# Another hand-ordered task list for sparse attention followed by a squared-ReLU MLP

## Chip, core and metric

The kernel runs on one core of one Trainium2 chip. The metric is the device time of one execution in microseconds (us), lower is better. The core's engines each work through their own instruction queue in order: TensorE (PE in the profile, its weight loads PEld), VectorE (DVE), ScalarE (ACT), GpSimd (POOL) and SyncE (SP, which here only issues DMAs). Engines wait for each other by semaphores.

## What is computed

```python
scores = scale * np.matmul(q, k.transpose(0, 1, 3, 2))      # q, k, v: 4 x 8 x 768 x 64, f32
mask = np.abs(blk_i - blk_j) <= window                      # blocks of 32 tokens, window 1
mask = mask | (blk_i == 0) | (blk_j == 0) | (blk_i == n_blocks - 1) | (blk_j == n_blocks - 1)
for qb in range(n_blocks):
    for kb in sampled_blocks[qb]:                           # 3 drawn blocks for each block of queries
        mask[qb * block:(qb + 1) * block, kb * block:(kb + 1) * block] = True
scores = np.where(mask, scores, -1000000000.0)
attn = np.exp(scores - np.max(scores, axis=-1, keepdims=True))
attn = attn / (np.sum(attn, axis=-1, keepdims=True) + 1e-09)
x = np.matmul(attn, v).transpose(0, 2, 1, 3).reshape(3072, 512)
h = x @ w_in                                                # 512 x 2048
r = np.maximum(h, 0.0)
out = (r * r) @ w_out                                       # 2048 x 512
```

## The kernel before

**Units and batches.** Two heads of one batch entry make a unit, so there are 16 units (0 to 15), four to a batch entry. Batches 0 and 1 (units 0 to 7) compute all scores and apply the mask; batches 2 and 3 (units 8 to 15) compute only the blocks that the mask keeps, for which drawn blocks of keys are copied together (`k_gather`) and drawn blocks of values are fetched from a copy in HBM (`v_store`, `v_gather`, `v_window`).

**Attention.** For a unit, q and k are loaded in f32 (`load`, line 145), cast to bf16 (`cast_qk`), and transposed: in batch 0 on PE (`transp`, then `evac` out of PSUM), from batch 1 on by a transposing DMA (`transp_dma`, line 311). `scores` makes the products of keys and queries in PSUM, `exps` the exponentials on ACT (line 360), `masks` multiplies by the mask on DVE (line 367), `values` multiplies by v on PE. `normalize` divides by the sum, and `x_transp` with `x_evac`, or a DMA, turns the result into columns. In batch 0 the first 256 queries of each unit have the mask added in PSUM instead, as a product of `oh` and `R2`; `R2` is made by `mask_rows` on PE (line 258) and copied by `mask_rows_evac`, and it needs the table `bm` (line 249).

**MLP.** The tokens go in 12 tiles of 256. For each, `hidden` makes 512 hidden columns at a time (f = 0, 4, 8, 12) in four parts, `relu` (line 727 on ACT, 729 on DVE) and `square` (738 on ACT, 740 elsewhere) follow, `output` sums over all hidden columns in eight parts, `out_copy` copies to SBUF and `store` writes to HBM. The last tile's rows are stored in four pieces.

**Weights.** `w_load` fetches w_in and w_out in four parts each with cast to bf16, by DMAs that GpSimd issues (lines 328 and 331). Hidden columns f need part f / 4 of w_in; output parts need w_out parts in turn. `loads_gate` (line 338) makes the sync queue wait for w_out parts 2 and 3 before it starts the loads of batch 1.

**Order.** All of this is a list of 1224 tasks, made in the program's order and numbered from 0. A string, `PROGRAM`, says in which order they are issued and on which engine: `P`, `V`, `A`, `G`, `S` for PE, DVE, ACT, GpSimd and the sync queue, then the task's number, and for a task that takes a cell of PSUM the cell (0 to 3). Semaphores follow from the data. So each engine's queue is the subsequence of its letter, and the place of a word among words of other letters says nothing. Buffers are handed out in rotation in the order of the words (8 for exponentials, 3 for relus, 12 for squares).

Numbers that matter here: 0, 2 `mask_rows`; 1, 3 `mask_rows_evac`; 4 to 17 `keep_warm` (products of ones, as filler); 21 `table_load`; 22 `table_places`; 73 and 52 `cast_v` of units 3 and 1; 74 to 77 `w_load` of w_in parts 0 to 3; 78 to 81 `w_load` of w_out parts 0 to 3; 82, 83 `loads_gate`; 102 the first `scores`; 253 to 283 loads, casts and transposes of batch 1; 285 to 291 the first `scores` of batch 1; 774 to 777 `hidden` f = 0 of the first tile and 778 its `relu`; 781 to 784 `hidden` f = 4 and 785 its `relu`; 802 to 809 the first tile's `output`; 1184 to 1223 the last tile's `output`, `out_copy` and `store`.

Of the kernel before, what the change touches and what calls it, by code (L numbers as in the profile page):

```python
# [25 lines left out]
def kernel(  # L26
# [65 lines left out]
    def run_program(bufs):  # L92
        names = {"P": "PE", "V": "DVE", "A": "ACT", "G": "POOL", "S": "SP"}
        taken = {name: [] for name in bufs}
        cells = [None] * NX
        for word in PROGRAM.split():
            t = tasks[int(word[1:].partition("/")[0])]
            if t.blocks and names[word[0]] in t.blocks[1]:
                wanted[names[word[0]]].append(t.blocks[0])
        for word in PROGRAM.split():  # L100
            i, _, spot = word[1:].partition("/")
# [951 lines left out]
```

## Time and profile before

| | |
|---|---|
| time, median of 3 runs (lowest, highest) | 258.85 us (258.25, 259.73) |
| the profiled execution | 258.04 us, span 256.3 us |
| granted clock of TensorE over the span | 1.0 |
| HBM read, written | 35.51 MB, 7.91 MB |

The page gives busy time by engine first. A window's row shows each engine's busy time in that stretch with the number of its instructions, then the clock, the mean share of the 16 DMA engines, and GB/s. In a timeline, a row is a start, a length and an instruction; the bracket holds the idle time of its engine before it and what ended it. Line 203 is a helper that issues most matmuls, and lines 121 and 123 are one that issues copies, so those rows are told apart by their tiles. Matmuls overlap: their mean length is a latency, not a pitch.

### The profile page before, as it was taken

Reading aid. Unit: us, or ns where it says so; the run is one execution under the profiler, and the core shown is the slowest. Engines: PE = TensorE matmul, PEld = TensorE weight load, DVE = VectorE, ACT = ScalarE, POOL = GpSimd, SP = SyncE. Lnnn points to the kernel's source line nnn. Section 1 sums busy time; section 2 is a strip of 40 time slices with the busy share of each in tenths; the row PEclk is TensorE's granted clock in tenths of the full one; section 3 lists DMA queues with packets and bytes.
Section 4 is the critical chain, followed back from the end, with each engine's and each line's share of the span. In section 5 each row is a group of like instructions: output and inputs, shape, how many; then the busy total and the mean of one; then the engine's idle time right before and its main releaser. Section 6 shows DMA issues by size and latency. Waiting matters only on the chain.

```text
span 256.3 us, 12057 instructions
## 1 busy us (share of the span) xinstructions
PE 244.4 (95%) x5265; PEld 183.4 (72%) x5265; DVE 173.0 (67%) x411; ACT 183.4 (72%) x217; POOL 100.3 (39%) x178
## 2 busy tenths in 40 slices
PE   7988999989999999998999999999999999999994
PEld 5667779759975579975866766857774677666674
DVE  7678997789998999869939647656636725730301
ACT  3799999978999799946695975585965186623640
POOL 3264228002407006198558424174448620413100
PEclk9999999999999999999999999999999999999999
DMA  6999998999799997999589899996484922034122
GB/s 191 364 246 205 206 208 128 252 255 241 190 262 232 207 239 141 313 217 201 191 232 207 226 170 212 251 190 186 115 203 98 195 47 50 16 102 145 46 84 84
DMA packets 64692, 47.08 MB, mean 184 GB/s; under 512 B 31567, under 2 KB 60624, under 8 KB 64640
## 3 DMA queue, kind: packets, MB, share of 16 engines
q1 hardware_dynamic: 58512, 37.82, 63.0%
q0 software_dynamic: 5440, 8.05, 16.9%
q8 instruction: 41, 0.67, 1.2%
q10 hardware_dynamic: 688, 0.46, 0.6%
q14 instruction: 11, 0.09, 0.2%
HBM read 35.51 MB, written 7.91 MB: 169 GB/s over the span
## 4 chain that ended last, share of the span: by engine, by line
PE 68%; DMA 16%; DVE 4%; POOL 4%; SPq 3%; issue 2%; ACT 1%; DVEq 0%; POOLq 0%
PE X L203 63%; DMA w_out_sb<-in_moe_w_out_dram 5%; PE X L673 5%; DMA ys<-in_v_dram 3%; DMA QKT<-qc 3%; DMA ks<-in_k_dram 2%; DMA qs<-in_q_dram 2%; DMA VG<-rows 1%; SPq L556 1%; POOL qc L123 1%; POOL w_in_sb L328 1%; SPq L560 1%; POOL VB L123 1%; ACT pT L643 1%; POOL g L740 1%
## 5 line engine op out<-in xcount | busy, mean ns | idle before, releaser
L203 PE MATMUL X<-xT,w_in_sb 64*128 64x256 bf16 x1536 | 100.0, 269 | 0.6 <-issue 0.4
L203 PE MATMUL X<-w_out_sb,g 64*128 64x512 bf16 (+3 forms) x960 | 95.4, 334 | 0.2
L203 PEld LDWEIGHTS <-w_in_sb 64*128 64x128 bf16 x1536 | 74.9, 94 | 12.3 <-issue 1.2
L360 ACT ACTIVATE pT<-X 128x1024 bf16<-128x1024 f32 x72 | 70.4, 1031 | 8.5 <-PE X L203 8.0
L203 PEld LDWEIGHTS <-g 64*128 64x128 bf16 x960 | 40.2, 94 | 26.7 <-issue 0.6
L643 ACT ACTIVATE pT<-X 128x768 bf16<-128x768 f32 (+1 forms) x56 | 41.5, 765 | 24.2 <-PE X L203 20.9
L740 POOL TENSOR_TENSOR g<-r 128x1024 bf16<-128x1024 f32 (+1 forms) x20 | 31.6, 1587 | 67.3 <-ACT r L727 50.0
L727 ACT ACTIVATE r<-X 128x1024 f32<-128x1024 f32 x28 | 29.8, 1070 | 20.6 <-PE X L203 16.9
L729 DVE TENSOR_SCALAR r<-X 128x1024 f32<-128x1024 f32 x20 | 24.5, 1224 | 26.9 <-POOL g L740 10.2
L367 DVE TENSOR_TENSOR pT<-pT,VG 128x1024 bf16<-128x1024 bf16 x60 | 41.5, 724 | 0.7 <-ACT pT L360 0.7
L738 ACT ACTIVATE g<-r 128x1024 bf16<-128x1024 f32 (+1 forms) x40 | 35.3, 901 | 2.7 <-DVE r L729 2.5
L203 PE MATMUL X<-QKT 64*128 64x256 bf16 (+1 forms) x384 | 32.9, 255 | 3.8 <-DMA QKT<-qc 1.2
L650 DVE TENSOR_TENSOR pT<-pT,MKS 128x768 bf16<-128x768 bf16 (+1 forms) x48 | 28.6, 629 | 8.7 <-ACT pT L643 8.6
L203 PEld LDWEIGHTS <-QKT 64*128 64x128 bf16 x384 | 16.9, 97 | 10.5 <-issue 4.4
L597 POOL DMA_INDIRECT VG<-rows,idx x19 | 21.2, 1118 | 4.6 <-issue 2.3
L203 PEld LDWEIGHTS <-pT 64*128 64x128 bf16 x768 | 16.1, 94 | 2.3 <-issue 0.3
L203 PE MATMUL X<-VB,pT 64*128 64x65 bf16 x768 | 17.4, 190 | 0.2 <-issue 0.2
L203 PEld LDWEIGHTS <-KG 64*128 64x128 bf16 x528 | 13.7, 95 | 5.0 <-issue 0.7
L203 PE MATMUL X<-QKT,KG 64*128 64x64 bf16 x528 | 15.3, 190 | 0.3 <-issue 0.2
L673 PEld LDWEIGHTS <-pT 128*64 128x64 bf16 x624 | 11.9, 111 | 5.0 <-issue 3.3
L679 DVE RECIPROCAL ss<-X 128x8 f32<-128x8 f32 x12 | 2.5, 206 | 18.8 <-PE X L673 16.8
L121 ACT COPY ys<-X 128x1024 f32<-128x1024 f32 (+1 forms) x10 | 9.7, 970 | 6.5 <-PE X L203 4.2
(107 smaller groups left out, 211.8 us busy)
## 6 DMA issues: line engine op xcount, KB each, us to landing
vs<-in_v_dram SPq DMA_DIRECT2D x14, 384.0 KB
ks<-in_k_dram SPq DMA_DIRECT2D x13, 384.0 KB
qs<-in_q_dram SPq DMA_DIRECT2D x12, 384.0 KB
out_dram<-ys SPq DMA_DIRECT2D x9, 512.0 KB
VG<-rows SPq DMA_DIRECT2D x20, 132.0 KB
w_in_sb<-in_moe_w_in_dram POOLq DMA_DIRECT2D x4, 512.0 KB, 8.8
w_out_sb<-in_moe_w_out_dram POOLq DMA_DIRECT2D x4, 512.0 KB, 9.5
rows<-VB SPq DMA_DIRECT2D x2, 792.0 KB
```

Of the source, the lines that this page charges most:

```text
L121: A.copy(out=out, in_=in_)
L203: last = nc.tensor.matmul(out(r ^ crossed), lhsT(r ^ crossed, rows), rhs(r ^ crossed, rows), skip_group_check=True, **kw)
L360: A.activation(out=pT[:, :, 0:n], in_=stile.pop(a)[:, :, 0:n], func=AF.Exp, scale=scale)
L367: V.tensor_tensor(out=pT, in0=pT, in1=m[:, None].broadcast_to([P, 2, len(cs), w]), op=AOP.mult)
L597: G.indirect_dma_start(out=to[0:RS * HB], out_offset=None, in_=pairs, in_offset=bass.IndirectOffsetOnAxis(ap=idx[0:RS * HB, g - 1:g], axis=0))
L643: A.activation(out=pT[:, :, 0:n], in_=stile.pop((u, v, gs))[:, :, 0:n], func=AF.Exp, scale=scale)
L650: V.tensor_tensor(out=pT, in0=pT, in1=m[:, None].broadcast_to([P, 2, n]), op=AOP.mult)
L673: nc.tensor.matmul(po[i * D:(i + 1) * D, h, a * VW:(a + 1) * VW], pts[g][:, h, c * D:(c + 1) * D], val, start=a == 0 and c == 0, stop=c == ...
L727: A.activation(out=to, in_=src, func=AF.Relu)
L729: V.tensor_scalar(out=to, in0=src, scalar1=0.0, scalar2=None, op0=AOP.max)
L738: A.activation(out=g, in_=r, func=AF.Square)
L740: (G if e == "POOL" else V).tensor_mul(out=g, in0=r, in1=r)
```

## The change

The string `PROGRAM` is replaced by another order of the same 1224 tasks. Nothing else differs. It was found by replaying orders with transfers and GpSimd work late by random amounts. 543 tasks are on PE in both; 93 tasks move between DVE, ACT, GpSimd and the sync queue:

| tasks | moves |
|---|---|
| `square` | 15 ACT to DVE, 11 GpSimd to ACT, 7 ACT to GpSimd, 3 GpSimd to DVE |
| `cast_qk` | 10 DVE to GpSimd, 2 GpSimd to DVE, 2 DVE to ACT, 1 GpSimd to ACT |
| `cast_v` | 3 DVE to GpSimd, 2 DVE to ACT, 2 GpSimd to ACT, 1 GpSimd to DVE |
| `relu` | 8 DVE to ACT, 8 ACT to DVE |
| `out_copy` | 5 ACT to DVE, 3 DVE to ACT |
| `x_evac`, `mask_evac` | 3 DVE to ACT, 1 ACT to DVE; 2 ACT to DVE |
| `v_gather` | 2 GpSimd to SP, 2 SP to GpSimd |

The first words on each queue (the word's letter is left out), before and after:

```text
PE    before  4 30 12 14 9 5 33 36 0 102 47 106 104 44 7 58 113 55 117 2 115 108
PE    after   0 2 4 30 12 14 9 5 33 36 102 47 106 104 44 7 58 113 55 117 115 108
DVE   before  32 31 111 1 34 209 46 48 43 45 54 59 56 67 3 64
DVE   after   3 1 32 31 111 34 209 46 48 43 45 54 59 56 67 64
ACT   before  29 37 103 107 105 114 118 116 128 124 126 134 138 60 87 136 177 171 147 150 174 190 97 785 184 144
ACT   after   29 37 103 107 105 114 118 116 128 124 126 60 134 138 87 136 177 171 147 150 184 174 190 97 785 187
POOL  before  35 57 41 75 76 52 38 74 73 49 77 81 80 787 78 794 793 79 256 801 22 258 280
POOL  after   35 57 41 22 75 81 38 49 77 76 52 74 80 73 78 79 787 780 793 258 264 800 266
SP    before  28 42 18 19 20 82 83 53 254 253 257 261 262 269 259 267 270 265
SP    after   18 19 20 21 83 28 42 82 53 253 254 261 262 269 259 255 257 277
```

On SP, 18 to 20, 28, 42 and 53 issue nothing. The diff itself, cut to the words around the first weights, the change to batch 1 and the end:

```diff
-    PROGRAM = """A29 G35 P4/3 V32 P30/0 P12/2 P14/3 P9/1 P5/1 V31 P33/1 V111 P36/3 P0/2 A37 V1 V34 P102/2
...
-P149/3 V172 P71/0 P141 V142 A150 V72 P50/2 P173/1 V148 P781/0 A174 P782 V178 P189/3 P783 V51 A190 V175 P90/1 P15/2 P96/2 P784 V91 A97 P183/3 V151 A785 P94/2 P179/1 V95 A184 G787 P143/0 P774/2 V180 P775 A144 V191 G78 P186/3 P181 P776 V182 A187 P777 V145 P157/0 V778 A786
...
-P205/2 V233 S265 A243 P225/1 P206 P805 V207 A226 S277 V274 P288/0 S436 S255 P208 P806 V227 A289 S275 V247 P11/1 P291/1 A823 P234/0 V241 P807 A292
...
-P1197 S1193 P1198 P1199 P1200 P1201 P13/1 P1204/1 P1205 V1202 P6/0 P1214/2 S1203 P1206 P1215 P1216 P1207 P1217 P1218 P1219 P1208 P1209 P8/3 P17/3 P1210 P1220 P1221 P1211 A1222 S1223 V1212 S1213"""
+    PROGRAM = """
+        P0/1 P2/0 S18 S19 S20 S21 A29 G35 P4/2 V3 V1 V32 P30/3 P12/2 P14/2 P9/0 P5/2 V31 P33/0 V111 P36/1 A37 V34 P102/2 V209 V46 P47/3
...
+        V142 V172 A150 P189/2 P183/3 P173/0 V148 P781/1 A184 A174 P186/3 P782 V178 P783 A190 V175 P90/0 P15/2 P96/2 P784 V91 P13/0 A97
+        V151 A785 P94/0 P179/2 V95 G78 G79 G787 P143/0 P774/1 V185 V180 P775 A187 A144 V188 V191 P181 P776 V182 P777 P163/0 P157/2 P8/3
+        V145 P11/3 P16/3 A786 P788/3 A778 A158 G780 P152/1 P789 P160/2 P790 V779 V153 P791 V159 A164 A161 V165 V162 P192/0 P154 P795/2
...
+        A243 P807 P205/2 P225/1 P808 P206 P239/0 G268 G817 A226 A240 S265 S267 S278 S438 S275 S273 S439 S446 S385 S279 V233 V244 V227
+        V207 P809 P234/1 P208 P291/0 V810 A210 A292 P235 P288/2 P830/3 P98/0 P831 V241 V236 P237 V99 A289 P298/2 P248/0 P249 V290 V250
...
+        P1209 P1188 P1214/0 P1189 P1190 P1191 P1210 P1211 P1195 P1215 P1216 P1196 P1217 P1197 P1218 P1219 V1192 S1155 P1220 A1212 S1193
+        P1221 P1198 V1222 P1199 P1200 S1213 P1201 V1202 S1223 S1203
+    """
```

47 lines of the change are left out of this document (46 added, 1 removed).

## Prediction

> **What bounds the kernel now.** I read the page's busy shares first, then the windows by stage, then the waits of PE.
>
> ```profile
> span 256.3 us, 12057 instructions
> PE 244.4 (95%) x5265; PEld 183.4 (72%) x5265; DVE 173.0 (67%) x411; ACT 183.4 (72%) x217; POOL 100.3 (39%) x178
> ```
>
> TensorE is busy for all but 11.9 us. No order of the same tasks can gain more than this idle time and what the matmuls lose by being issued loosely. The windows (length; busy time and count of PE, weight loads, DVE, ACT, POOL; clock; DMA share; GB/s) tell where that lies.
>
> ```profile
> 0.00:29.00 29.00, 24.77 (x454) 18.72 (x456) 22.05 (x59) 22.21 (x26) 11.44 (x27) 1.00 1.02 247
> 29.00:51.65 22.65, 22.56 (x480) 18.27 (x476) 19.00 (x35) 22.31 (x28) 8.78 (x17) 1.00 1.10 194
> 51.65:57.10 5.45, 4.25 (x92) 2.96 (x94) 4.55 (x11) 3.97 (x6) 0.00 (x0) 1.00 0.97 291
> 57.10:252.90 195.80, 192.78 (x4247) 143.43 (x4243) 127.08 (x307) 134.73 (x160) 80.05 (x135) 1.00 0.76 173
> ```
>
> PE idles 4.23 us in the first 29, 1.20 at 51.65, 3.02 in all the time from 57.1 to 252.9, and about 3.4 behind that while the last rows are stored. From 29 to 51.65 ACT is busy 22.31 of 22.65 us: there the exponentials set the pace, and PE only just follows. So three places count: the start, the change from batch 0 to batch 1 near 52, and many small waits behind it.
>
> The wait at 51.65 is one wait in the timeline (start, length, instruction, idle time before it), and the chain of waits (start, length, step) says what was late:
>
> ```profile
> 52.85 0.40 PE L203 MATMUL X<-QKT 64*128 64x256 bf16 x4 [1.20 <-DMA QKT<-qc]
> 53.28 1.02 ACT L360 ACTIVATE pT<-X 128x1024 bf16<-128x1024 f32 x1 [1.48 <-PE X L203]
> ```
>
> ```profile
> 21.48 13.02 DMA w_out_sb<-in_moe_w_out_dram
> ...
> 34.51 0.24 SPq L338
> ...
> 35.20 4.66 DMA ks<-in_k_dram
> ...
> 44.60 8.11 DMA QKT<-qc
> ```
>
> The sixth weight load lands at 34.50, the gate on the sync queue (line 338) opens, batch 1's first keys land 4.66 us later, a cast on POOL and a transposing DMA of 8.11 us follow, and PE starts batch 1 at 52.85.
>
> **The change part by part.** No task is added or removed: 543 PE tasks in both, so PE's matmul work is a wash, and on PE a task moves by 7 places of 543 on average. What changes is who waits for whom.
>
> *Weight loads (GpSimd queue).* Before, the six loads go out as w_in parts 1, 2, 0, 3, then w_out parts 3, 2; after, as w_in 1, w_out 3, w_in 3, 2, 0, then w_out 2, 0, 1. Part 0 of w_in goes from third place to fifth. It is needed second: task 774 (hidden columns f = 0) still follows task 781 (f = 4).
>
> ```profile
> 14.90 1.76 POOL L328 DMA_DIRECT2D w_in_sb<-in_moe_w_in_dram  x2
> ...
> 17.96 0.77 POOL L328 DMA_DIRECT2D w_in_sb<-in_moe_w_in_dram  x1
> ...
> 20.75 1.52 POOL L331 DMA_DIRECT2D w_out_sb<-in_moe_w_out_dram  x2
> ```
>
> ```profile
> 18.00:32.00 14.00, 12.95 (x288) 10.79 (x289) 12.79 (x29) 13.43 (x17) 6.05 (x9) 1.00 1.24 206
> w_in_sb<-in_moe_w_in_dram POOLq DMA_DIRECT2D x4, 512.0 KB, 8.8
> ```
>
> The issues end at 22.27, but the transfers run at a flat 206 GB/s: 524 KB by 206 GB/s is 2.55 us each. The sixth lands at 34.50, so the fifth at 31.95 and the third at 34.50 − 3 × 2.55 = 26.85; the third's issue end (18.73) plus 8.8 gives 27.5, which agrees. So time to landing grows with the place in the queue (8.8 for the third, 13.02 for the sixth), and part 0, fifth, lands at about 31.95.
>
> When does PE come to task 774?
>
> ```profile
> 28.91 1.04 PE L203 MATMUL X<-xT,w_in_sb 64*128 64x256 bf16 x16
> ```
>
> ```profile
> 27.46 1.03 ACT L727 ACTIVATE r<-X 128x1024 f32<-128x1024 f32 x1
> 28.36 2.93 ACT L360 ACTIVATE pT<-X 128x1024 bf16<-128x1024 f32 x3
> ```
>
> Before, at 28.91, with part 0 there for 2 us. After, it takes the PSUM cell of task 781, whose relu (the 27.46 row, ending 28.49) stands one exponential later (2.93 / 3 = 0.98): 29.47 at the earliest, up to 1.3 later by the later start below. The wait is 31.95 − 29.47 = 2.5 at most and 1.2 at least; I take +2.0. In-order PE has everything else queued behind it, and ACT's task 778, the relu of those columns (moved from DVE to ACT), holds the exponentials behind it in turn.
>
> The Trainium skill's page "DMA: Bandwidth & Descriptors", section "Queues, rings and completion order", has each DMA engine take descriptors in ring order, with one ring for each pair of queue row and engine; by that rule a load's place decides its landing, and the sum keeps its +2.0. Read instead as a fixed 8.8 us from issue, this row would put part 0 at about 29.3 in the new order, and the sum would be 2.0 lower.
>
> *Start.* PE does both mask-row products (tasks 0, 2) ahead of the first transposes, and DVE both their copies (3, 1) ahead of the second key cast (32).
>
> ```profile
> 4.16 0.18 DVE L249 TENSOR_SCALAR bm<-r 24x48 bf16<-24x48 f32 x1
> 4.50 0.55 DVE L123 CAST qc<-ks 128x384 bf16<-128x384 f32 x1 [0.17 <-DMA ks<-in_k_dram]
> 4.97 0.35 DVE L123 COPY QKT<-X 128x384 bf16<-128x384 bf16 x1
> 5.37 0.40 PE L258 MATMUL X<-oh,bm 64*128 64x256 bf16 x1
> 5.81 0.42 DVE L123 CAST R<-X 128x256 bf16<-128x256 f32 x1 [0.49 <-PE X L258]
> 6.29 0.40 PE L203 MATMUL X<-QKT 64*128 64x256 bf16 x2 [0.52 <-DVE R L123]
> L123 DVE CAST R<-X 128x512 bf16<-128x512 f32 x1 | 0.7, 683 | 0.0
> ```
>
> bm is ready at 4.34; two products end near 5.2; copies of 0.68 and 0.42 end near 6.25; cast (0.55), transposes and two copies out of PSUM (0.35 each) put the first scores near 7.6 in place of 6.29: 1.3 later. It only moves the arrival within the wait for part 0, so it adds 0; without that wait it would cost up to 1.3.
>
> *Batch 1's loads, casts and transposes.* After, SP issues five loads in one run behind the gate, where before transposes waiting on casts stood between them; ten casts of q and k move from DVE to POOL.
>
> ```profile
> L123 POOL CAST qc<-ks 128x768 bf16<-128x768 f32 x2 | 1.6, 823 | 17.2 <-PE X L203 17.0 <-DMA ks<-in_k_dram 0.2
> L123 POOL CAST qc<-qs 128x768 bf16<-128x768 f32 x1 | 1.2, 1177 | 0.1
> L203 PE MATMUL X<-w_out_sb,g 64*128 64x512 bf16 x704 | 87.7, 376 | 0.1
> ```
>
> Batch 1 has five of the ten: 4 to 6 us by 823 to 1177 ns, and POOL is idle 13.87 of the 22.65 us before 51.65, which hides them; without that room each would put its transposes about 1 us back. PE also has four more output parts (806 to 809) ahead of the first scores of batch 1, 32 matmuls by 87.7 / 704 = 0.125 us, 4.0 us of cover. The wait for QKT should go: −1.2 (bounds −1.2 and 0). PE, once late, also has its exponentials done ahead: of what it loses to ACT's pace from 29 to 57 I let it regain 0.7 (bounds 0 and 1.0).
>
> *Engines.* DVE gets 18 squares, 5 output copies, 8 relus and 2 mask copies, and gives away casts, 8 relus and 3 copies: about 11 us more. No row shows a square on DVE; it lies between the 724 ns of a bf16 product (line 367) and the 1224 of an f32 relu (line 729), and I take 1.2, the f32 case.
>
> ```profile
> L367 DVE TENSOR_TENSOR pT<-pT,VG 128x1024 bf16<-128x1024 bf16 x60 | 41.5, 724 | 0.7 <-ACT pT L360 0.7
> L729 DVE TENSOR_SCALAR r<-X 128x1024 f32<-128x1024 f32 x20 | 24.5, 1224 | 26.9 <-POOL g L740 10.2
> L727 ACT ACTIVATE r<-X 128x1024 f32<-128x1024 f32 x28 | 29.8, 1070 | 20.6 <-PE X L203 16.9 <-DVE pT L650 3.6
> ```
>
> Behind 57.1 DVE is idle 68.7 of 195.8 us, so this hides; where a relu is the one PE waits for, it costs 0.15 more on DVE than ACT's 1070.
>
> *Everything behind 57.1.*
>
> ```profile
> PE X L673 <- DMA VG<-rows: 0.4, 1, 0.4
> ```
>
> Its whole idle time is 3.02 us: with all of it gone −3.0, with as many new waits +3.0. Transposes, gathers and windows are issued further ahead of their use; only 0.4 of this idle time ends on a DMA, so I take −0.3.
>
> *Tail.*
>
> ```profile
> 250.59 0.42 DVE L123 COPY qs<-X 128x256 f32<-128x256 f32 x1 [6.83 <-PE X L203]
> ...
> 252.13 0.28 PE L203 MATMUL X<-warm 64*128 64x128 bf16 x4
> 252.98 0.29 DVE L123 COPY qs<-X 128x128 f32<-128x128 f32 x1 [1.97 <-PE X L203]
> 253.31 0.37 ACTq L796 DMA_DIRECT2D out_dram<-qs  x1
> ```
>
> The last copy is the 256-column one (0.42 for 0.29) with twice the bytes to store, about +0.3; four pairs of filler products leave the tail (the 252.13 row shows two of them, 0.28 with their latency), about −0.2. Net +0.1.
>
> **Sum**, on the profiled execution (258.04, span 256.3): +2.0 − 1.2 − 0.7 − 0.3 + 0.1 = −0.1, so 257.9. That execution lies 0.8 below the median of 258.85, so 258.7 for the median: no change.
>
> **Rivals.** *Faster.* The wait for part 0 costs nothing, because PE is that late in any case or regains it while ACT is full. The 2.0 falls away, and half of the 3.02 goes: 258.04 − 1.2 − 0.7 − 1.5 + 0.1 = 254.7, median 255.5. For it: leads of the DMAs grow nearly everywhere. Against: part 0 has a landing time that no PE work moves, and few waits end on DMAs.
>
> *Slower.* ACT, not PE, paces the kernel until batch 0 is done. At task 774 it loses the full 2.5 and, at 98% busy, can regain nothing; the QKT wait then hides under ACT's lateness and returns nothing. 258.04 + 2.5 + 0.1 = 260.6, median 261.4. For it: the ACT row above. Against: up to there ACT has 51 tasks after and 52 before, and ACT stood idle 1.48 us at the old wait. It decides at the last exponentials of batch 0 (51.80 before): beyond 54 the rival holds.
>
> *The change does little*, because PE hardly waits for what it makes safer, is the forecast itself.
>
> **Numbers.** Forecast 0.36, faster 0.31, slower 0.33. Half a per cent is about what a measurement here tells from no change, 257.6 to 260.1; that is the forecast's own range. The extremes of all bounds are 258.04 − 5.2 and + 5.9 (medians 253.6 and 264.7); I leave the outer part of each rival out: 254.8 to 262.4.
>
> **What would show it.** A PE wait of 1.2 to 2.5 us near 30 ended by the DMA of w_in; first scores near 7.6; no wait on QKT near 52; the first scores of batch 1 at 57 to 58.5 (52.85 + 4.0 and up to 1.6 of lateness); idle time of PE behind that near 2.7. I am wrong if part 0 lands before PE comes, or if idle time behind 57 moves by more than 2.

## The result, and the profile after

| | before | after |
|---|---|---|
| median (lowest to highest), 4 runs each, one chip | 258.55 us (257.86 to 259.73) | 276.21 us (274.74 to 278.81) |
| ratio | 1 | 1.069 (95% interval 1.060 to 1.078) |
| profiled execution, span | 258.04, 256.3 | 274.74, 272.9 |

The changed kernel is 17.7 us slower; the forecast was 258.7, with 262.4 as the upper end. The page after, its span and its busy shares (busy time, share, instructions):

```profile
span 272.9 us, 12061 instructions
PE 246.8 (90%) x5265; PEld 183.8 (67%) x5265; DVE 186.8 (68%) x411; ACT 179.3 (66%) x214; POOL 105.7 (39%) x181
```

The span grew by 16.6 us. PE's idle time (span less busy) grew from 11.9 to 26.1, which is 14.2 of them; PE's busy time grew by 2.4 with the same 5265 matmuls, which are issued more loosely. The granted clock (0.998 over the span, 1.0 before) does not explain the difference. The same four windows as before say where the idle time is:

```profile
0.00:29.00 29.00, 21.11 (x402) 15.86 (x404) 19.70 (x54) 19.92 (x23) 13.78 (x37) 1.00 1.05 256
29.00:51.65 22.65, 20.78 (x384) 16.68 (x381) 19.84 (x33) 20.17 (x25) 9.52 (x9) 1.00 1.05 241
51.65:57.10 5.45, 4.73 (x108) 3.45 (x106) 3.79 (x6) 2.45 (x4) 1.93 (x2) 1.00 1.60 280
57.10:252.90 195.80, 183.73 (x4007) 135.25 (x4005) 137.29 (x312) 132.74 (x158) 77.41 (x130) 1.00 0.67 160
```

By length less PE's busy time, with before's value behind it: 7.89 (4.23), 1.87 (0.09), 0.72 (1.20), 12.07 (3.02). Together with what lies behind 252.9 (3.55 for 3.4) these make the 14.2. The windows hold unlike work in the two kernels, since after is late, but they show the kind of loss: nine of fourteen microseconds lie where the forecast had room for 3. ACT, which filled 22.31 of the 22.65 us before 51.65, now fills 20.17: it no longer paces that stretch.

What PE waits for (total, times, longest), after, and under it the rows of before that answer to it:

```profile
PE X L203 <- ACT pT L360: 5.2, 12, 1.0
PE X L203 <- DVE pT L367: 3.2, 3, 1.8
PE X L203 <- DVE XS L413: 3.1, 3, 1.7
PE X L673 <- issue: 2.3, 5, 0.5
PE X L427 <- DVE xq L413: 1.2, 2, 0.7
PE X L203 <- DVE bm L192: 1.2, 1, 1.2
PE X L203 <- DVE r L729: 1.2, 1, 1.2
```

```profile
PE X L203 <- DMA QKT<-qc: 1.2, 1, 1.2
PE X L203 <- ACT pT L360: 0.3, 1, 0.3
PE X L203 <- DVE XS L413: 0.3, 1, 0.3
```

Of before's rows the one for QKT, which the change was to remove, is gone. In its place PE waits for ACT and DVE. (The row for `bm` is the first wait of the program; before has the same 1.2 us under another name.) A row such as "X, line 203, waits for pT, line 360" reads in two ways: the exponentials make pT, but they also empty the PSUM cell X that PE wants next.

PE's timeline after, at the places that the forecast named (start, length, instruction, idle time before it and what ended it):

```profile
7.67 0.29 PE L203 MATMUL X<-QKT 64*128 64x256 bf16 x2 [0.47 <-ACT QKT L121]
...
32.15 0.39 PE L203 MATMUL X<-QKT 64*128 64x256 bf16 x4
32.38 1.04 PE L203 MATMUL X<-xT,w_in_sb 64*128 64x256 bf16 x16
...
49.72 0.39 PE L203 MATMUL X<-QKT 64*128 64x256 bf16 x4 [1.18 <-DVE r L729]
...
55.24 0.23 PE L427 MATMUL X<-identb,xq 64*128 64x64 bf16 x4 [0.72 <-DVE xq L413]
...
62.95 0.54 PE L203 MATMUL X<-VB,pT 64*128 64x65 bf16 x24 [1.77 <-DVE pT L367]
...
63.61 0.39 PE L203 MATMUL X<-QKT 64*128 64x256 bf16 x4
```

First scores at 7.67; task 774 at 32.38 with no wait on a DMA; then three waits on DVE of 0.7 to 1.8 us, and the first scores of batch 1 at 63.61.

Which of the two meanings a wait has can be told by replaying the string: it says which task emptied the cell that a word takes, and which tasks made its data, and the trace says which ended last. Over all gaps of PE above 0.06 us this gives (worked out from the traces, us):

| PE gaps that end on | before | after |
|---|---|---|
| a PSUM cell not yet emptied | 2.4 | 11.4 |
| data | 1.1 | 5.7 |
| anything else | 3.5 | 4.0 |

So the waits for cells grew by 9.0 us and those for data by 4.6. What stands in the cells shows it too: in the two batches with full scores, finished scores wait in PSUM for their exponential for 16.7 us in sum before and 29.6 after (in the sampled batches it is 35.1 and 25.4), and finished hidden columns for their relu 13.3 and 23.7.

The written strings seem to say why: of the words that take a PSUM cell, 32 before and 93 after do so when, by the order of the words, all but one of the four cells are still held. But the place of a word among words of other letters binds nothing. With the words of the other engines set as far ahead as their own queues and the data allow, the same queues give 5 and 10; and before's order with the new engines, told below, counts 32 like before and has 14.9 us of waits for cells. So this count is no measure of the loss.

How late after is along the way can be read at equal work: the time at which PE has done a given share of all matmul work (columns weighted by the part of the array they use). Three experiments, told below, are set beside it: i1 is after's order behind the first 44 us of before's, h3 is before with four parts of the change put in, k2 is after with three repairs.

| share of work | before | after | i1 | h3 | k2 |
|---|---|---|---|---|---|
| 10% | 35.9 | 39.4 | 34.8 | 37.1 | 40.1 |
| 20% | 60.5 | 68.1 | 62.1 | 62.2 | 66.4 |
| 30% | 84.0 | 93.6 | 85.9 | 85.3 | 92.7 |
| 40% | 107.8 | 120.4 | 116.6 | 112.3 | 119.1 |
| 50% | 133.4 | 149.7 | 143.8 | 137.9 | 146.7 |
| 80% | 206.5 | 223.7 | 214.5 | 209.2 | 220.3 |
| 100% | 252.9 | 269.3 | 260.1 | 255.6 | 265.9 |

After loses 3.5 us in the first tenth, 4 in the second, 9 from there to the middle, and almost nothing behind it (16.3 late at 50%, 16.4 at the end). So the loss lies in the batches with full scores and in the change to the sampled ones (the last full scores end at 107.1 and 119.9, the first sampled ones start at 109.1 and 126.5); the half with sampled scores and gathers runs at before's pace.

### The profile page after: what moved, and what is told of

It reads as the page before. It is cut to its first block, busy times and chain, and to the rows that moved or that the text cites. A ratio compares the mean times of both kernels' runs of the same rounds, so it can differ in the third digit from the quotient of the medians.

```text
span 272.9 us, 12061 instructions
## 1 busy us (share of the span) xinstructions
PE 246.8 (90%) x5265; PEld 183.8 (67%) x5265; DVE 186.8 (68%) x411; ACT 179.3 (66%) x214; POOL 105.7 (39%) x181
## 4 chain that ended last, share of the span: by engine, by line
PE 46%; DVE 4%; issue 2%; DVEq 2%; SPq 1%; another core or an unknown queue 1%; DMA 1%; ACT 0%
PE X L203 41%; PE X L673 5%; DVEq L571 2%; DVE KG L618 1%; DVE pT L367 1%; DMA VG<-rows 1%; SPq L799 1%; DVE XS L682 1%; DVE r L729 0%; SPq L560 0%; ACT pT L643 0%; SPq L686 0%; SPq L801 0%; DVE pT L650 0%
## 5 line engine op out<-in xcount | busy, mean ns | idle before, releaser
L203 PE MATMUL X<-xT,w_in_sb 64*128 64x256 bf16 x1536 | 101.2, 269 | 0.9 <-ACT pT L360 0.4
L203 PE MATMUL X<-w_out_sb,g 64*128 64x512 bf16 (+3 forms) x960 | 94.1, 334 | 0.0
L367 DVE TENSOR_TENSOR pT<-pT,VG 128x1024 bf16<-128x1024 bf16 x60 | 48.2, 841 | 2.3 <-ACT pT L360 2.2
L729 DVE TENSOR_SCALAR r<-X 128x1024 f32<-128x1024 f32 x20 | 24.2, 1219 | 27.3 <-PE X L203 23.7
L740 POOL TENSOR_TENSOR g<-r 128x512 bf16<-128x512 f32 (+1 forms) x13 | 19.9, 1539 | 56.3 <-ACT r L727 46.4
L203 PE MATMUL X<-QKT 64*128 64x256 bf16 (+1 forms) x384 | 31.2, 250 | 6.8 <-ACT pT L360 2.9
L650 DVE TENSOR_TENSOR pT<-pT,MKS 128x768 bf16<-128x768 bf16 (+1 forms) x48 | 24.5, 548 | 6.0 <-ACT pT L643 6.0
L738 ACT ACTIVATE g<-r 128x1024 bf16<-128x1024 f32 (+1 forms) x29 | 24.6, 867 | 4.0 <-DVE r L729 3.8
L740 DVE TENSOR_TENSOR g<-r 128x1024 bf16<-128x1024 f32 (+1 forms) x18 | 19.8, 1106 | 9.0 <-ACT r L727 8.8
L203 PEld LDWEIGHTS <-QKT 64*128 64x128 bf16 x384 | 16.6, 95 | 12.6 <-issue 8.9
L123 POOL CAST qc<-qs 128x384 bf16<-128x384 f32 (+3 forms) x20 | 14.5, 743 | 21.3 <-DMA QKT<-qc 15.8
L612 POOL COPY KG<-QKT 128x256 int32<-128x256 int32 x10 | 5.4, 536 | 38.7 <-PE X L203 25.5
```

What stands on the lines that cost most here:

```text
L123: (V if e == "DVE" else G).tensor_copy(out=out, in_=in_)
L203: last = nc.tensor.matmul(out(r ^ crossed), lhsT(r ^ crossed, rows), rhs(r ^ crossed, rows), skip_group_check=True, **kw)
L367: V.tensor_tensor(out=pT, in0=pT, in1=m[:, None].broadcast_to([P, 2, len(cs), w]), op=AOP.mult)
L650: V.tensor_tensor(out=pT, in0=pT, in1=m[:, None].broadcast_to([P, 2, n]), op=AOP.mult)
L729: V.tensor_scalar(out=to, in0=src, scalar1=0.0, scalar2=None, op0=AOP.max)
L738: A.activation(out=g, in_=r, func=AF.Square)
```

## The experiments

Each ratio is against runs of the kernel before on the same chip (medians there 255.1 to 258.9); after itself, run as a control, is at 1.0626. Words are those of the string.

**Order or engines?** The diff has two halves that can be parted: the order of the words, and their letters. 89 of the moved tasks can keep either letter in either order (the four gathers that change queue stay with their order). First the new order on the old engines:

```diff
-A778 ... G780 ... V779 ... A794 ... V256 ... G264 ... G266 ... G274
+V778 ... A780 ... A779 ... G794 ... G256 ... V264 ... V266 ... V274
```

> The changed kernel's order of words, with the engines of before for 89 of the 93 moved tasks (the four v_gather stay as changed). Theory, GpSimd beside VectorE: the masks (line 367) lengthen wherever GpSimd computes at the same time (0.68 us alone, 1.0 beside it), and the casts and squares that the change gave GpSimd between 40 and 64 us make the waits of TensorE at 48.5, 54.5 and 61.2 us (1.18, 0.72, 1.77). With the engines of before the mean of line 367 falls from 841 to about 720 ns, these three waits lose at least 2 of their 3.7 us, and the time is 271 to 273.5. Rival, the order alone: the waits come from the order in the queues, line 367 changes but the time stays at 275 to 277.

Measured 296.31 us, 1.167 (1.156 to 1.177): 41 us slower, far outside what either theory gave, although the masks did get shorter (a mean of 760 ns on line 367, 841 in after). PE's gaps for cells are 27.1 us here. TensorE's granted clock was at half for 20.5 us of this execution (0.964 over the span), which costs some 10 us of the 41 at most. Then the old order on the new engines:

```diff
-V778 ... A779 ... G794 ... A780 ... G256 ... V266
+A778 ... V779 ... A794 ... G780 ... V256 ... G266
```

> The order of before, with the changed kernel's engines for the same 89 tasks. Theory, GpSimd beside VectorE: the mean of line 367 rises from 724 to 800 ns or more, and the time to 262 to 266. Rival, the order alone: 258 to 260, since VectorE and GpSimd have idle time for the moved tasks in the order of before.

Measured 273.34, 1.078 (1.066 to 1.089), 18 us slower, again beyond both theories; the mean mask takes 814 ns (724 in before), and PE's gaps for cells grow from 2.4 to 14.9 us. So the letters alone cost as much as the whole change, and the order alone more than twice as much. The two halves don't add up; each order fits only its own engines. In particular, that the moved tasks hide in the idle time of the engines that get them is refuted, for all 89 together, in before's own order. Which of the 89 something waits for was not parted.

**Single suspects, taken out of after.** The start first, the first 52 words of before and then the rest of after:

```diff
-        P0/1 P2/0 S18 S19 S20 S21 A29 G35 P4/2 V3 V1 V32 P30/3 ...
+        A29 G35 P4/2 V32 P30/3 ... P36/2 P0/1 A37 V1 V34 ... P2/0 V67 A118 P115/1 V3 ...
```

> The first 52 words of before (mask rows behind the first transposes again), the changed order behind them. Theory, a late start is carried to the end: first scores back from 7.67 to 6.3 us and the time 1.3 to 3 us shorter, 273 to 275. Rival, it is swallowed by later waits, as the prediction had it (counted 0): 275.5 to 277.

Measured 272.87, 1.070 (1.056 to 1.084): no gain shows. In the profiled execution the second half of unit 0's keys landed late (its cast on DVE starts at 5.82 us, 4.50 in before), so its profile doesn't show the start undisturbed, and the interval is some 3.6 us to either side, so a gain of 2 us could hide in it. Whether an earlier start alone is swallowed stays open.

Then the row numbers of the first gathers. Task 25 reads a table into DVE's registers (line 571); DVE's queue reaches these loads when the work issued ahead of them has run out:

```profile
L571 DVEq TENSOR_LOAD <-tab x2: 1809/1947/2085, 96.1 to 98.0; - x2
```

```profile
L571 DVEq TENSOR_LOAD <-tab x2: 2215/3206/4197, 112.1 to 114.4; - x2
...
113.25 0.22 DVE L528 TENSOR_SCALAR idx<-X,lane 128x11 int32<-128x11 f32 x1
118.79 0.18 DVE L410 RECIPROCAL rs<-X 128x4 f32<-128x4 f32 x1 [5.31 <-ACT g L738]
```

The first fence is before, the second after (shortest, median and longest in ns, first and last start; then DVE's timeline). The loads are no "busy" work, they belong to the queue; yet from 113.5 to 118.8 DVE does nothing, and PE waits three times near there (0.95 at 118.5, 0.70 at 121.6, 1.70 at 124.8). In before, 4 us of work issued ahead of the same two loads run on DVE meanwhile. Putting task 25 right behind task 26 gives after that cover too:

```diff
-V27 V26 V398 ... V885 V25
+V27 V26 V25 V398 ... V885
```

> The changed kernel with task 25 (table_rows and the register loads behind it on VectorE, GpSimd and the sync queue) moved forward by seven words of VectorE, right behind task 26, as close to it as in the order of before. Theory, the register loads stop VectorE's queue unless work stands ahead of them: the idle time of VectorE from 113.5 to 118.8 us (5.3) falls to 3.5 or less and TensorE's waits near 118.5, 121.6 and 124.8 (0.95, 0.70, 1.70) shrink by 1 us or more in sum; time 273.5 to 275.5. Rival, VectorE's stop is hidden: time 275.5 to 277.

Measured 270.99, 1.064 (1.051 to 1.077). The profile shows the mechanism: the idle time falls from 5.31 to 2.40, and at 60% of the work the kernel is 3.6 us ahead of the control (169.7 for 173.3):

```profile
112.26 1.90 DVE L367 TENSOR_TENSOR pT<-pT,VG 128x1024 bf16<-128x1024 bf16 x3 [2.40 <-ACT r L727]
```

At the end it is 1.3 ahead, and the ratio is the control's. Some of the gain goes into a wait for a gather that is now the late one, and some of the difference is the clock: it was at half for 3.41 us from 106.7 in the control's execution and from 219.3 in this one.

```profile
217.89 0.89 PE L673 MATMUL X<-VG,pT 128*64 128x65 bf16 x45 [1.92 <-DMA VG<-rows]
```

**The same suspects, one at a time, put into before.** There a small loss is not swallowed by a larger one. Six of the casts that moved from DVE to GpSimd:

```diff
-V266 ... V264 ... V274 ... V272 ... V282 ... V260
+G266 ... G264 ... G274 ... G272 ... G282 ... G260
```

> The kernel before, with six casts (266, 264, 274, 272, 282 of q and k, 260 of v) moved from VectorE to GpSimd at their places in the order. GpSimd stands idle there from 44.6 to 61.6 us. Theory, GpSimd beside VectorE: the masks (line 367) between 45 and 64 us lengthen from 0.68 to 1.0 to 1.3 us wherever a cast runs beside them, VectorE gains nothing from being rid of six casts of 0.55, the mean of line 367 rises from 724 to 770 ns or more, and the time is between no change and 2.5 us more. Rival, as the prediction had it: idle GpSimd hides the casts, VectorE is 3.3 us less busy, and the time stays or falls by up to 1 us.

Measured 257.18, 1.0045 (0.9997 to 1.0092), an interval that reaches no change. The masks did not get longer on average (718 ns for 724); the theory had 770 or more. Task 25 behind task 411, which takes its cover:

```diff
-V25 P928 V411
+P928 V411 V25
```

> The kernel before, with two neighbours in VectorE's queue swapped: task 25 (table_rows with the register loads behind it) stands behind task 411 (a normalize that waits for TensorE) instead of ahead of it. Theory, register loads stop the queue unless issued work stands ahead of them: before they run from 96.1 to 100.0 us behind 4 us of work that is already issued; now they cannot begin until 411's wait ends near 100.7, VectorE stands idle about 3.3 us (3.9 less 411's 0.64), and the time is 1.5 to 3.5 us longer. Rival: VectorE has room there, and the time stays within 0.5 us.

Measured 259.15, 1.0126 (1.0025 to 1.0228). DVE's timeline and PE's waits show the hole of after, made in before:

```profile
100.36 0.22 DVE L528 TENSOR_SCALAR idx<-X,lane 128x11 int32<-128x11 f32 x1
...
105.05 1.29 DVE L367 TENSOR_TENSOR pT<-pT,VG 128x1024 bf16<-128x1024 bf16 x2 [4.47 <-issue]
```

```profile
PE X L203 <- DVE pT L367: 2.6, 1, 2.6
```

The weight loads in after's order:

```diff
-G75 ... G76 ... G74 ... G77 ... G81 ... G80 ... G78 ... G79
+G75 ... G81 ... G77 ... G76 ... G74 ... G80 ... G78 ... G79
```

> The kernel before, with the eight weight loads in the changed kernel's order in the same places of GpSimd's queue (w_in 1, w_out 3, w_in 3, 2, 0, w_out 2, 0, 1). As the prediction had it: part 0 of w_in lands near 32, TensorE waits 2 to 3 us for it at task 774 (28.9), time 2 to 3 us longer. Rival: TensorE does not wait, or regains it, as in the changed kernel, where no wait near 30 is ended by a weight load: within 0.5 us.

Measured 260.25, 1.0173 (1.0056 to 1.029). PE's waits:

```profile
PE X L203 <- DMA w_in_sb<-in_moe_w_in_dram: 2.1, 1, 2.1
...
PE X L398 <- POOL VB L123: 1.5, 1, 1.5
```

This is the forecast's wait for part 0, 2.1 us for a predicted 2.0, from 30.93 to 33.04. The close agreement is luck in part: PE came and the load landed each over a microsecond later than forecast (29.47 and 31.95). GpSimd's first weight load went out 1.2 us later in this execution than in before (16.08 for 14.90), and TensorE's clock was at half for 3.41 us from 19.3 and again from 33.0. The second row, a wait for a cast of v at 18.7, comes of that late queue: the same number of issues stands ahead of the cast in both orders. So the edit's own share of the 4.4 us is not parted from these. And the two mask-row products first:

```diff
-A29 G35 P4/3 V32 ... P36/3 P0/2 A37 V1 ... P2/1 V67 A118 P115/2 V3
+A29 G35 P0/2 P2/1 P4/3 V3 V1 V32 ... P36/3 A37 ... V67 A118 P115/2
```

> The kernel before, with both mask-row products ahead of the first transposes on TensorE and both copies ahead of task 32 on VectorE, as in the changed kernel. Theory, a late start is carried to the end: first scores at 7.6 instead of 6.3 us, time 1 to 2 us longer. Rival, it is swallowed: within 0.5 us.

Measured 256.99, 1.0078 (1.0029 to 1.0127), first scores at 7.70: a start 1.4 later costs 2.0 us in before (0.78% of 256, with an interval from 0.7 to 3.3).

**All together, in both directions.** After with the casts back on DVE and two squares off GpSimd; then that with the start, the weights' order and task 25 put back as well; then before with all four single parts:

```diff
-G264 G266 G274 G260 G272 G282 G800 G817
+V264 V266 V274 V260 V272 V282 A800 A817
```

> The changed kernel, with six casts (264, 266, 274, 272, 282, 260) moved from GpSimd back to VectorE and two squares (800, 817) from GpSimd back to ScalarE, at their places in the changed order. Theory, GpSimd beside VectorE: the masks between 44 and 63 us, of which six took 1.3 to 2.4 us, are back at 0.68 to 0.9, TensorE's waits of 1.18, 0.72 and 1.77 us at 48.5, 54.5 and 61.2 lose 2 us or more in sum, and the time is 2 to 4 us shorter than the changed kernel's. Rival: VectorE, which gets 3.3 us of casts in return, is as late as before, and the time moves by less than 1 us.

Measured 271.67, 1.0636 (1.0566 to 1.0705), no gain, though the profile shows what the edit does. The masks of line 367 between 44 and 63 us (shortest, median, longest in ns), first before, then after, then this kernel:

```profile
L367 DVE TENSOR_TENSOR pT<-pT,VG x14: 680/686/1157, 45.1 to 62.6; 128x1024 bf16<-128x1024 bf16 x14
```

```profile
L367 DVE TENSOR_TENSOR pT<-pT,VG x11: 678/1304/2380, 44.6 to 61.6; 128x1024 bf16<-128x1024 bf16 x11
...
45.50 1.28 POOL L123 CAST qc<-qs 128x768 bf16<-128x768 f32 x1
...
58.85 2.27 POOL L740 TENSOR_TENSOR g<-r 128x1024 bf16<-128x1024 f32 x1 [4.76 <-DVE r L729]
```

```profile
L367 DVE TENSOR_TENSOR pT<-pT,VG x11: 680/681/691, 46.8 to 61.0; 128x1024 bf16<-128x1024 bf16 x11
```

With GpSimd computing beside them the masks take 1.30 in place of 0.68 us, once 2.38, and GpSimd's own work gets longer in places (1.28 for two of its casts of 128 x 768 between 44 and 63 us, where most of that size took 0.82 or 0.83). Relieved, the masks are back at 0.68, and the three waits of PE near 49, 55 and 63 shrink from 1.18, 0.72 and 1.77 to 0.60, 0.23 and 0.30. The 2.5 us so won don't reach the end. The Trainium skill's page "SBUF — State Buffer", section "SBUF: two separate sides", says that VectorE and GpSimd share one pair of ports, which one instruction holds to its end while the other engine blocks, among other cases when the VectorE instruction has two inputs in SBUF, as a mask has, and the GpSimd one reads SBUF. The rows agree that it is these two, and that a mask is lengthened by most of a cast (0.62 for 0.82). They don't tell a lock from a shared rate, as both sides got longer.

> The changed kernel itself, as it is, beside the next three on one chip. Both theories: the ratio of its first measurement, 1.069 (1.060 to 1.078).

The control, after itself: 272.13, 1.0626 (1.0551 to 1.0701).

```diff
-        P0/1 P2/0 ... V3 V1 ... G75 G81 ... G77 G76 ... G74 ... V885 V25
+        A29 G35 ... P0/1 ... V1 ... P2/0 ... V3 ... G75 G76 ... G74 ... G77 G81 ... V26 V25 V398
```

> The changed kernel with four parts undone at once: the first 52 words of before, the weight loads in the order of before (and the gate on w_out 3 behind the gate on w_out 2 on the sync queue), the casts and squares of h1_gpsimd_relieved, and task 25 right behind task 26. Theory, these four are most of the loss: ratio 1.02 to 1.04. Rival, the loss lies in the order of everything else (scores and hidden products on TensorE, loads far ahead on the sync queue): ratio 1.05 or more.

Measured 269.06, 1.0545 (1.0477 to 1.0612): all four parts undone give back 3 of 17 us by the medians, with intervals of the two ratios that overlap, though PE's gaps for cells and for data fall to 6.9 and 4.0 (control 9.9 and 5.9).

```diff
+G266 G264 G274 G272 G282 G260
+P928 V411 V25
+G75 ... G81 ... G77 ... G76 ... G74
+P0/2 P2/1 P4/3 V3 V1
```

> The kernel before with the four parts that were measured alone (casts on GpSimd, 25 behind 411, weight loads in the changed order, mask rows first) put in at once. Alone they cost 1.2, 3.2, 4.4 and 2.0 us. Theory, each stops TensorE at another place and nothing behind gives time back: they add up to 9 to 12 us, ratio 1.035 to 1.047. Rival, a late TensorE makes the later waits shorter, so they overlap: 4 to 7 us, ratio 1.016 to 1.028.

Measured 262.66, 1.0289 (1.0216 to 1.0362): put into before, they cost 7.1 us by the medians, 7.4 by the ratio. (Alone they cost 1.2, 3.2, 4.4 and 2.0 by their ratios, in sum 10.8, so they overlap.) By these two measurements the four explain some 3 to 7 of the 17 us; 10 to 14 lie elsewhere in the order and its engines.

**Is the rest a late start that goes on?** The first 243 words of before, to about 44 us, then after's order:

```diff
-        P0/1 P2/0 S18 S19 S20 S21 A29 G35 ...
+        A29 G35 P4/2 V32 P30/0 ... P821 V213 S21 P13/0 P8/3 ... V198 P802/3 V822 P245/1 ...
```

> The first 243 words of before (up to about 44 us), the changed order behind them. In the changed kernel TensorE is 3.7 us late at that point and 16.5 at the end. Theory, each stretch of the changed order loses time by itself: 11 to 13 us stay, ratio 1.043 to 1.052. Rival, the late start is what makes the later stretches wait: less than 8 us stay, ratio below 1.03.

Measured 265.55, 1.0441 (1.0321 to 1.0561). The early part is worth 5 to 6 us, but 10 stay, and the table above shows them arise anew: 1.6 late at 20% of the work, 10.4 at 50%. The windows (44 to 90, 90 to 133), after and then this kernel:

```profile
44.00:90.00 46.00, 40.55 (x914) 30.76 (x911) 43.11 (x64) 35.03 (x40) 23.53 (x24) 1.00 0.96 207
90.00:133.00 43.00, 37.77 (x821) 26.82 (x819) 31.65 (x92) 34.12 (x40) 12.66 (x19) 1.00 0.88 215
```

```profile
44.00:90.00 46.00, 43.03 (x918) 30.25 (x917) 39.79 (x85) 36.55 (x42) 20.39 (x24) 1.00 1.21 241
90.00:133.00 43.00, 35.60 (x817) 28.32 (x813) 29.03 (x69) 30.45 (x35) 14.17 (x29) 0.96 0.93 213
```

PE idles 7.40 us from 90 to 133 in this kernel, more than after's 5.23 there, with all other engines less busy than PE (the clock's 0.96 there is one stretch of 3.41 us at half). So the later stretch loses by itself; its order and its engines are not parted here.

**Is it DVE's length?** From 44 to 90 DVE is busy 43.11 of 46 us in after. Eight of its relus there are made on half of the columns, in after and in before (the other columns keep old values):

```diff
-            V.tensor_scalar(out=to, in0=src, scalar1=0.0, scalar2=None, op0=AOP.max)
+            half = slice(0, 1) if T in ((0, 256, 256), (0, 512, 256)) else slice(0, 2)
+            V.tensor_scalar(out=to[:, half] if T[0] < SB else to, in0=src[:, half] if T[0] < SB else src, ...)
```

> The changed kernel, with the relus of tiles 1 and 2 that run on VectorE (all eight) done on half their columns, so that 8 times 0.53 = 4.3 us of VectorE's work between 43 and 90 us are left out (the other half keeps old values). Theory, VectorE paces that stretch in the changed order (busy 31.7 of the 32.9 us from 57.1 to 90): time 2.5 to 4.5 us shorter than the changed kernel's, ratio to before 1.045 to 1.055. Rival, TensorE's own order and the cells of PSUM it takes cause the waits, whatever VectorE has to do: ratio 1.06 or more.

Measured 270.52, 1.067 (1.056 to 1.078): no gain. In the windows from 57 to 90 of the control and of this kernel DVE is relieved, and PE is not:

```profile
57.00:90.00 33.00, 29.65 (x722) 22.70 (x720) 31.25 (x44) 25.63 (x30) 17.17 (x18) 1.00 0.92 195
```

```profile
57.00:90.00 33.00, 29.40 (x724) 22.16 (x720) 28.89 (x49) 26.35 (x30) 15.10 (x16) 1.00 0.98 200
```

> The same cut in the kernel before, where five of these relus run on VectorE (2.7 us of its work left out). Theory, VectorE does not pace that stretch there (ScalarE and VectorE share it, 30.1 and 30.4 of 32.9): 0 to 0.7 us shorter. Rival, VectorE's length counts in any order: 1.5 to 2.7 us shorter.

Measured 253.69, 1.0009 (0.9961 to 1.0057): nothing in before either. In this stretch DVE's busy time is not what holds PE.

**Is it the choice of the cell?** A word names its cell. In 187 words of each string another cell is taken, of those that are free by the order of the words the one that the trace shows emptied first; only the figure behind the stroke changes:

```diff
-P4/3 ... P30/0 ... P9/1 ... P5/1 ... P33/1 ... P36/3
+P4/0 ... P30/1 ... P9/0 ... P5/2 ... P33/3 ... P36/0
```

> The kernel before with the order kept and the PSUM cells chosen anew: at each word that takes a cell, of those that are free there the one that is drained first by the times of the profile (187 words get another cell). Theory, part of TensorE's small waits and loose issue is a cell that is not yet drained (0.45 at 14.8, 0.30 at 16.8, 0.37 at 24.0): 0.5 to 2 us shorter than before. Rival: the choice among free cells matters to nobody, within 0.5 us.

Measured 255.38, 1.0047 (0.999 to 1.0103).

```diff
-P0/1 P2/0 ... P9/0 ... P33/0 ... P36/1
+P0/0 P2/1 ... P9/1 ... P33/1 ... P36/0
```

> The changed kernel with the order kept and the PSUM cells chosen anew by the rule of i5_before_cells (187 words). In the changed kernel 9.9 of TensorE's 19.6 us of waits are for a cell that is not yet drained, against 2.4 before. Theory, which cell is taken matters: 2 us or more of these waits go, time 1.5 to 3 us shorter than the changed kernel's, ratio to before 1.050 to 1.058. Rival, the order of the words leaves no better cell (at 93 of the 266 words that take one, only one cell is free; before at 32): within 1 us, ratio 1.059 to 1.069.

Measured 276.97, 1.0639 (1.0534 to 1.0743). No gain in either, and the gaps for cells stay near the control's 9.9 (8.9). The rule chose only among cells that are free by the written order, which is narrower than the queues need. Wait by wait in after's trace, another of the four cells had been emptied earlier for 4.6 of the 11.4 us, and none for the other 6.8. So by this count a freer choice of cells could touch less than half of these waits; it was not tried. The rest needs another order, or other engines for the tasks that empty the cells.

Finally everything that had shown an effect in a profile, in after: task 25 early, GpSimd relieved, the cells:

```diff
-V885 V25 ... G264 G266 G274 G260 G272 G282 G800 G817 ... P0/1 P2/0
+V26 V25 ... V264 V266 V274 V260 V272 V282 A800 A817 ... P0/0 P2/1
```

> The changed kernel with three things at once: task 25 right behind task 26 (as e4_rows_early), six casts and two squares off GpSimd (as h1_gpsimd_relieved), and the cells chosen anew for that. Theory, they act at different places and add up: 5 to 8 us shorter than the changed kernel's, ratio 1.030 to 1.045. Rival, the order of the scores, hidden products and their drains keeps the rest: ratio 1.05 or more.

Measured 272.77, 1.0554 (1.0477 to 1.063), about 1% better than the changed kernel with new cells alone (1.0639) on the same chip, with intervals that overlap; gaps for cells 6.7, for data 4.2. None of these kernels beats before.

## Why the prediction was wrong, step by step

**The step that failed** is "Everything behind 57.1": "its whole idle time is 3.02 us: with all of it gone −3.0, with as many new waits +3.0 ... I take −0.3". The bound +3.0 was made by mirroring the small idle time of before, and nothing in that idle time limits what another order can add: before's 3.02 is what its own order and engines leave. Measured it is 12.07 in the same window, and at equal work after loses 8.7 us between 20% and 50%. The reasons given for −0.3 looked at DMAs alone, since "only 0.4 of this idle time ends on a DMA" and transfers were issued further ahead; the waits that came are on PSUM cells and on data from DVE. No term of the sum stood for the emptying of the cells.

That the waits for cells grew by 9 us is shown by the traces, and both halves of the change show it alone (14.9 us with the new engines, 27.1 with the new order). Which moves make the cells empty late, and so cause the 10 to 14 us that the four parts leave, stays open. It is what remains after an earlier start (worth 5 to 6 us with all of the first 44 us), DVE's length and the choice among cells were each tried; it was not shown by a repair. Putting back before's order or engines in one stretch behind 44 us was not tried, nor was a cell added.

**"Behind 57.1 DVE is idle 68.7 of 195.8 us, so this hides"** failed by the same reasoning: these are a mean over unlike stages, and idle time says nothing of who waits for the moved task. Old order with new engines, DVE's among them, was 18 us slower. As to sizes, DVE grew by 13.8 us where about 11 was forecast, and about half of that is the masks' lengthening:

```profile
L367 DVE TENSOR_TENSOR pT<-pT,VG 128x1024 bf16<-128x1024 bf16 x60 | 48.2, 841 | 2.3 <-ACT pT L360 2.2
L740 DVE TENSOR_TENSOR g<-r 128x1024 bf16<-128x1024 f32 x14 | 17.1, 1225 | 6.8 <-ACT r L727 6.6 <-issue 0.2
L740 DVE TENSOR_TENSOR g<-r 128x512 bf16<-128x512 f32 x4 | 2.7, 689 | 2.2 <-ACT r L727 2.2
```

The masks' 48.2 stands against 41.5 before; a whole square on DVE took 1.23 for the 1.2 assumed (four of the 18 are of half the size), so its price was right.

**"POOL is idle 13.87 of the 22.65 us before 51.65, which hides them"**, for the casts: GpSimd did have the room, but in after its work beside VectorE's has a cost (0.68 to 1.30 us for a mask), which six of the casts in before's order did not have on average. Its effect on the whole time is small: 1.0045 in before, not clear of no change, and none seen in after.

**"It only moves the arrival within the wait for part 0, so it adds 0"**, on the start: first scores came at 7.67 as predicted (7.6), but 1.4 us later at the start cost 2.0 us in before, and by task 774 PE was 3.5 late, since from 0 to 32 it also waits for exponentials to empty the cells that its scores, mask tiles and filler take, where before had one such wait of 0.3 in all (for its transposes both have 0.7 to 0.8 more):

```profile
PE X L203 <- ACT pT L360: 3.3, 7, 0.9
```

**Part 0 of w_in.** Landing by place in the queue fits: with after's order of loads in before, part 0 does land behind PE, and PE waits 2.1 (2.0 predicted, at times a microsecond earlier). (The forecast's own check adds 8.8 to the end of an issue; the profile counts it from the start, which gives 26.8 for the third load and agrees better with its 26.85.) In after there was no wait, because PE was later than the load. The issue's row and its DMAs' time to landing in after:

```profile
L328 POOL DMA_DIRECT2D w_in_sb<-in_moe_w_in_dram x4: 745/761/976, 13.1 to 19.3; - x4
...
DMA to landing us min/median/max: 8.1/9.9/11.1
```

Part 0 is the last of the four, issued at 19.3, so with the longest of these times it was there by 30.4 (31.95 forecast; GpSimd's first load went out at 13.1, 14.9 in before), and PE came at 32.38. This is the case that the forecast named as its refutation, for a reason that it didn't have.

**The QKT wait** is gone, as predicted (−1.2). **"Of what it loses to ACT's pace from 29 to 57 I let it regain 0.7"** had the wrong sign: PE lost 1.78 more from 29 to 51.65. The first scores of batch 1 came at 63.61, not 57 to 58.5. **The tail** is right to 0.1 or so (+0.1 forecast; from PE's last matmul to the end of the span 3.6 us for 3.4).

**The slower rival** had the sign and its test (the last exponentials of batch 0 beyond 54; they end at 61.43), but not the mechanism. ACT's timeline after:

```profile
57.09 1.02 ACT L360 ACTIVATE pT<-X 128x1024 bf16<-128x1024 f32 x1 [2.31 <-PE X L203]
58.98 1.02 ACT L360 ACTIVATE pT<-X 128x1024 bf16<-128x1024 f32 x1 [0.86 <-PE X L203]
60.41 1.02 ACT L360 ACTIVATE pT<-X 128x1024 bf16<-128x1024 f32 x1 [0.41 <-PE X L203]
```

ACT waits for PE ahead of each of the last exponentials, while PE's gaps end on ACT and DVE: the wait goes round between them, and ACT is not the pace. Register loads (task 25) were in no term at all; they cost 1.3% (0.3 to 2.3) in before where they have no cover.

## What to carry to other kernels

An engine that is idle for a third of a long stretch is no cover for work that is moved to it, and the small idle time of a well-fitted order is no bound on what a new order can lose. Ask of each word that takes a PSUM cell or a buffer which task empties it, on which engine, and what stands ahead of that task in its queue. Ask it of the queues, with times: a count from the written order of all words together also depends on how the queues are interleaved in writing. An order and its choice of engines are fitted to each other, so price them together, and look in each in-order queue for the slow steps that are nobody's busy time, such as register loads. When single repairs each show their effect in the profile and none in the time, stop adding up waits and look for the shared resource that hands the delay on.

## What the runs showed of the hardware

- Two register loads on DVE's queue took 1.8 and 2.1 us in before, and 2.2 and 4.2 in after, where DVE ran dry behind them for 5.31 us.
- GpSimd computing beside VectorE's bf16 products made these 0.68 to 1.30 us long, once 2.38 beside a square of 2.27.
- PE can stop in the middle of a group of matmuls that, by the profile, waits for nobody. In the kernel with half relus in the changed order:

```profile
67.37 0.51 PE L203 MATMUL X<-xT,w_in_sb 64*128 64x256 bf16 x6
69.65 0.28 PE L203 MATMUL X<-xT,w_in_sb 64*128 64x256 bf16 x2 [1.77 <-issue]
```

  After with GpSimd relieved has one of 1.06 us at 67.2. One packet of instructions was fetched between 65 and 71 us in the first of these; whether the stop is that fetch was not tried.

- TensorE's granted clock fell to half for 3.41 us at a time, 22 times in 12 of the 20 profiled executions (once for twice as long), apart from the end of the program. Each time PE had been busy for 2.1 us or less of the 3.41 just before. Of before and after as first measured neither shows it; the control shows it twice, once in this window, with PE busy 3.50 of 5 us:

```profile
105.00:110.00 5.00, 3.50 (x40) 2.79 (x38) 2.52 (x7) 3.46 (x4) 2.28 (x9) 0.67 0.38 61
```

  So a few waits close together can cost some 1.7 us more of TensorE's time (half of 3.41, an estimate), and leads of that size between two single profiles can be due to it.
